# Attention to mixture-of-experts kernel: token rows stored in parts, routing parts moved behind a copy, fills and splits issued later, decay rows on two queues

## The chip, the core and the metric

The kernel runs on one core of one Trainium2 chip. The core has a matrix engine (TensorE, PE in the profile; its weight loads are PEld), a vector engine (VectorE, DVE), an activation engine (ScalarE, ACT), GpSimd (POOL) and a sync engine (SyncE, SP) that mostly issues DMA transfers. Each engine works off its own instructions in order and waits on semaphores for the others. Sixteen DMA engines move data between HBM, SBUF (on-chip memory of 128 partitions) and, for copies between partitions, from SBUF to SBUF. TensorE writes to PSUM. The metric is the device time of one execution in microseconds; less is better.

## What is computed

Attention with a decay, over 4 batches of 8 heads, 576 tokens, head dimension 64; then a mixture of 8 experts in which each token takes the one expert of its largest logit; then a dense feed-forward pair with a leaky ReLU.

```python
scores = scale * np.matmul(q, k.transpose(0, 1, 3, 2))
cum = np.cumsum(np.log(np.clip(f, 0.0001, 1.0)), axis=-1)
decay = cum[:, :, :, None] - cum[:, :, None, :]
scores = np.where(causal, -1000000000.0, scores + decay)
attn = np.exp(scores - np.max(scores, axis=-1, keepdims=True))
attn = attn / (np.sum(attn, axis=-1, keepdims=True) + 1e-09)
x = np.matmul(attn, v)                       # to (2304, 512): tokens x (heads, dim)
logits = x @ w_gate + modality_bias[modality_id]
e_idx = np.argmax(logits, axis=1)            # gate_w: softmax weight of that expert
out[mask] = gate_w[mask, None] * (np.maximum(x[mask] @ w1[e], 0.0) @ w2[e])
h = out @ w_in                               # 512 x 2048
return np.maximum(0.01 * h, h) @ w_out       # 2048 x 512
```

## The kernel before

Everything is float32 in and out. TensorE works on a rounded form (fp32r); where precision is needed a tile is split into a high part, which ScalarE casts, and a low part, which VectorE subtracts, and a product is three products.

**Attention** works on 16 pairs of heads (g = 0 to 15), four pairs to a batch. The queries are cut into five chunks c of up to 128 rows. A loop over the pairs writes the instructions of TensorE, ScalarE, VectorE and SP in a fixed order (`ordered(tc, MS)`), in four steps per pair: `first` (scores of chunks 0 and 1 of pair g, transposes of chunk 3 of pair g-1, and the lower half of the operands of pair g+1, `prep_lo`), `last` (scores of chunk 4; transposes of chunk 4 and the first value product `pv` of pair g-1), `third` (scores of chunk 2, the second value product of pair g-1, transposes of chunks 0 and 1) and `fourth` (scores of chunk 3, loads for later pairs, the upper half of the operands of pair g+2, `prep_hi`, transposes of chunk 2, and `xout`, which brings the result of pair g-1 to token rows). What is moved by DMA per pair, all issued by SP and in this order: the raw q and k (`raw`, L197), v (`vt`, L188), decay rows (L295, L296), `bk<-aq` (L297), `bq<-raw` (L308), `ak<-raw` (L309) and `aq<-aq` (L310). The last four shift halves between partitions; `aq<-aq` overwrites the half that `bk<-aq` of the same pair reads.

A value product writes the one PSUM tile of the pool `psv` (L420); VectorE copies it out (`xu`, L431) before the next value product may write it. The transposed probabilities go through the pool `pst`, three PSUM tiles in turn, which ScalarE empties into `tt` (L405, L415).

**Routing** of a batch starts when its fourth pair is through `xout`. `route` (L462) is a generator: each `next` writes a few small VectorE instructions (largest logit, one-hot `oall`, ranks, gate weight), and `routed(n)` takes n such pieces at fixed places in the steps: three in `last` ahead of the value product, three in `third`, one behind `fourth`, and one more in each of the two steps for g > 12. The last piece stores the batch's token rows (512 values and the reciprocal of the gate sum) to `xs` in HBM, in two DMAs of 1026 and 128 KB (L531, L532).

**The start** (`start`, L219) makes the cumulated decay `agt` on VectorE (L255, L256, L259), copies its rows into the operands of pair 0 by four small DMAs of SP (L263) and stores it for the other pairs (`agd`, L264). GpSimd meanwhile fills buffers of later pairs with constants (L272 to L284).

**Experts.** 25 slots of 128 tokens are gathered from `xs` by expert; `split` (L832) makes high and low parts of the weights of a slot and issues the load of the next slot's. The splits of the first slot (`split(0, 0, k)`, L1042) and the first transposes of tokens (`trx(0)`, L1043) are written ahead of the expert loop, and a scheduler places them among the last attention instructions; `issue_after(lasts[-1].ins)` lets it place the splits behind the last copy of transposes of chunks 0 and 1. **The dense pair** follows (`g1`, `g2`).

Of the kernel before, what the change touches and what calls it, by code (L numbers as in the profile page):

```python
# [73 lines left out]
def fused(ctx: ExitStack, tc, qk0, qk2, vp, f, mid, wg, mb, w1, w2, w_in, w_out, out):  # L74
# [66 lines left out]
    with tc.tile_pool(name="pst", bufs=PST, space=PSUM) as pst:  # L141
# [77 lines left out]
        def start():  # L219
# [40 lines left out]
            for t, r0, c0 in ((bq, 64, 0), (bk, 66, 2)):  # L260
                for i in range(2):
                    o = t[r0 + i:r0 + i + 1].rearrange("r h s -> r (h s)").rearrange("r (p j) -> r p j", p=8)
                    nc.sync.dma_start(o.bitcast(F32), agt[0:8, c0 + i, :].bitcast(F32))  # L263
            nc.sync.dma_start(agd.rearrange("c h (s j) -> (h s) c j", s=4), agt.bitcast(F32))  # L264
            nc.vector.tensor_sub(ak[64:128, 0], kr[64:128, 0], ak[64:128, 0].bitcast(F32))
            nc.vector.scalar_tensor_tensor(bq[0:64, 0], qr[0:64, 0], 0.125, aq[0:64, 0].bitcast(F32), ALU.mult, ALU.subtract)
# [5 lines left out]
            for t in aq4[1:] + bq4[1:]:  # L272
                nc.gpsimd.memset(t.bitcast(F32), 0.0)
            for t in bq4[1:]:
                nc.gpsimd.memset(t[64:68, :, :64].bitcast(F32), 1.0)
            for t in bqs[1:] + bks[1:]:
                nc.gpsimd.memset(t[64:68].bitcast(F32), 1.0)
            nc.gpsimd.memset(idw, 0.0)
            nc.gpsimd.memset(midi, 0)
            nc.gpsimd.tensor_copy(idw[:, :, 0:P], ident.unsqueeze(1).to_broadcast([P, H // 2, P]))  # L280
            nc.gpsimd.tensor_copy(aq4[0][:, :, :64], aq[:, :, 4 * P:].bitcast(F32))
            nc.gpsimd.tensor_copy(bq4[0][:, :, :64], bq[:, :, 4 * P:].bitcast(F32))
            for t in p4s:
                nc.gpsimd.memset(t[:, S:], 0.0)  # L284
# [52 lines left out]
        def exps(g, c, view, nm, pt):  # L337
            for j in range(2):
                nc.scalar.activation(pt[:, j, :], view[:, j, :], AF.Exp, bias=nm[:, j:j + 1], scale=1.0, accum_out=sms[g % 3][:, c, j:j + 1])  # L339
            st[g, c, "p"] = pt  # L340
# [121 lines left out]
        def route(b):  # L462
# [67 lines left out]
            t0 = b * S  # L530
            nc.sync.dma_start(xs[t0:t0 + 4 * P, :].rearrange("(c p) d -> p c d", p=P), x[:, 0:4, :])  # L531
            nc.sync.dma_start(xs[t0 + 4 * P:t0 + S, :], x[:64, 4, :])  # L532
# [91 lines left out]
        lasts = []  # L624
# [7 lines left out]
        def first(g):  # L632
            then = qk01(g) if g < NG else None
            cs = [tr(g - 1, 3, (j, )) for j in range(2)] if g else ()
            if g + 1 < NG:
                prep_lo(g + 1)
            for c in cs:
                c()
# [3 lines left out]
        def last(g):  # L642
            then = qk4(g) if g < NG else None
            if g:
                tr(g - 1, 4, (0, 1))
                routed(3 + (g > 12))
                pv(g - 1, 0)
            if then:
                then()

        def third(g):
# [4 lines left out]
            if then:  # L656
                cs = [tr(g, c, (0, 1)) for c in range(2)]
                then()
                for c in cs:
                    lasts.append(c())  # L660
# [128 lines left out]
    with tc.tile_pool(name="rt2", reuse_waits="tile", bufs=1) as rt2, \  # L789
# [250 lines left out]
        with tc.issue_after(lasts[-1].ins):  # L1040
# [138 lines left out]
```

## Time and profile before

| what | value |
| --- | --- |
| median of 3 runs | 914.2 us (913.07 to 915.13) |
| profiled execution | 911.09 us |
| its span | 909.4 us |
| TensorE busy | 863.0 us (95%) |
| VectorE busy | 629.2 us (69%) |
| ScalarE busy | 526.4 us (58%) |
| GpSimd busy | 141.9 us (16%) |
| mean granted TensorE clock | 0.987 |

All durations below are of the profiled execution, in microseconds from the start of its span. Attention fills roughly the first 230 us, the experts the time up to about 500 us, the dense pair the rest. A line of a timeline names the start, the length, the engine (SPq is SP's DMA queue, the length there is that of the issue), the line of the program, the operation, and the tiles, output first. In brackets stands how long the engine was idle before and what released it. PEclk is the granted clock of TensorE as a share of full speed.

### The profile page before, as it was taken

How to read it: one execution, taken by the hardware profiler on the slowest of the kernel's cores; microseconds unless marked ns; L12 is line 12 of the kernel's file. 1: busy time of each engine (PE TensorE's matmuls, PEld its weight loads, DVE VectorE, ACT ScalarE, POOL GpSimd, SP SyncE). 2: the span in 40 equal slices, each digit the busy share in tenths (PEclk: the TensorE clock that was granted, in tenths of full speed). 3: DMA queues.
4: the chain of work that ended last, by engine and by line, in shares of the span. 5: the costliest groups of instructions: out<-in, count | busy, mean ns of one | idle time of the engine just before them, and what ended most of it. 6: DMA issues, size and time to landing. Idle time of an engine off the chain costs nothing. (4 is left out here: it accounts for less than half of the span.)

```text
span 909.4 us, 14373 instructions
## 1 busy us (share of the span) xinstructions
PE 863.0 (95%) x4733; PEld 710.0 (78%) x4733; DVE 629.2 (69%) x1091; ACT 526.4 (58%) x993; POOL 141.9 (16%) x181
## 2 busy tenths in 40 slices
PE   5999899898979999999999999999999999999995
PEld 3877777776758788888877888888888888888885
DVE  6677768588899999999987364368336943473333
ACT  5877767577768899999986353354223422232221
POOL 5000000000112324454532100000000000001112
PEclk9999999999999999999999999999999999999998
DMA  5776867758338516422231232024000400011111
GB/s 154 221 175 166 210 162 176 200 120 276 74 98 281 155 42 188 132 70 70 84 103 38 83 94 81 1 70 114 2 1 25 136 27 0 1 47 47 47 47 69
DMA packets 32962, 92.91 MB, mean 102 GB/s; under 512 B 7317, under 2 KB 7989, under 8 KB 32882
## 3 DMA queue, kind: packets, MB, share of 16 engines
q1 hardware_dynamic: 28082, 76.71, 29.6%
q0 software_dynamic: 4800, 15.23, 5.3%
q8 instruction: 39, 0.64, 0.3%
q14 instruction: 41, 0.34, 0.1%
HBM read 132.09 MB, written 14.99 MB: 162 GB/s over the span
## 5 line engine op out<-in xcount | busy, mean ns | idle before, releaser
L1085 DVE SCALAR_TENSOR_TENSOR us<-u,us 128x512 f32<-128x512 f32 (+1 forms) x80 | 51.0, 637 | 126.2 <-ACT us L1084 125.6
L1084 ACT COPY us<-u 128x512 f32<-128x512 f32 (+1 forms) x80 | 43.5, 544 | 162.8 <-PE u L1082 162.7
L1082 PE MATMUL u<-fxl,whii 128*128 128x512 f32 (+1 forms) x320 | 118.1, 369 | 0.0
L1082 PE MATMUL u<-fxh,wloi 128*128 128x512 f32 (+1 forms) x320 | 117.9, 368 | 0.0
L1082 PE MATMUL u<-fxh,whii 128*128 128x512 f32 (+1 forms) x320 | 116.8, 369 | 0.7 <-ACT fxh L740 0.7
L1102 PE MATMUL a<-whio,gh 128*128 128x512 f32 x288 | 112.8, 392 | 0.0
L1102 PE MATMUL a<-wloo,gh 128*128 128x512 f32 x288 | 112.3, 390 | 0.0
L1102 PE MATMUL a<-whio,gl 128*128 128x512 f32 x288 | 106.0, 390 | 0.0
L835 DVE TENSOR_TENSOR w1l<-w1r,w1h 128x1024 fp32r<-128x1024 f32 x84 | 100.8, 1221 | 4.6 <-ACT w1h L834 4.1
L835 DVE TENSOR_TENSOR w2l<-w2r,w2h 128x1024 fp32r<-128x1024 f32 x80 | 94.4, 1217 | 0.9 <-ACT w2h L834 0.7
L834 ACT CAST w1h<-w1r 128x1024 fp32r<-128x1024 f32 x84 | 85.8, 1054 | 2.3 <-PE h L854 2.2
L339 ACT ACTIVATE p<-sc,nm 128x128 f32<-128x128 f32 (+3 forms) x128 | 66.1, 526 | 31.3 <-DVE nm L334 28.4
L834 ACT CAST w2h<-w2r 128x1024 fp32r<-128x1024 f32 x80 | 81.4, 1051 | 2.8 <-PE y L882 2.2
L1088 ACT CAST gh<-us 128x512 fp32r<-128x512 f32 (+1 forms) x80 | 46.2, 578 | 58.7 <-DVE us L1085 39.4
L1089 DVE TENSOR_TENSOR gl<-us,gh 128x512 fp32r<-128x512 f32 (+1 forms) x80 | 50.9, 636 | 39.8 <-ACT gh L1088 39.0
L334 DVE TENSOR_REDUCE nm<-sc 128x2 f32<-128x256 f32 (+1 forms) x64 | 51.1, 819 | 30.0 <-PE sc L328 22.5
L882 PE MATMUL y<-w2h,hl 128*128 128x512 f32 x160 | 64.0, 400 | 5.5 <-DVE hl L875 5.4
L1112 POOL DMA_INDIRECT out<-acc,tid x18 | 17.9, 995 | 327.2 <-DVE acc L1109 290.1
L1082 PEld LDWEIGHTS u<-fxh,whii 128*128 128x128 f32 x320 | 60.2, 188 | 11.1 <-ACT fxh L740 0.9
L1082 PEld LDWEIGHTS u<-fxh,wloi 128*128 128x128 f32 x320 | 60.3, 188 | 10.4
L1082 PEld LDWEIGHTS u<-fxl,whii 128*128 128x128 f32 x320 | 60.3, 188 | 10.2
L882 PE MATMUL y<-w2h,hh 128*128 128x512 f32 x160 | 65.3, 408 | 0.0
(263 smaller groups left out, 1839.4 us busy)
## 6 DMA issues: line engine op xcount, KB each, us to landing
w1r<-w SPq DMA_DIRECT2D x88, 512.0 KB
w2r<-w SPq DMA_DIRECT2D x82, 512.0 KB
rwi<-w_in SPq DMA_DIRECT2D x16, 512.0 KB
rwo<-w_out SPq DMA_DIRECT2D x16, 512.0 KB
raw<-qk SPq DMA_DIRECT2D x14, 576.0 KB
vt<-vp SPq DMA_DIRECT2D x16, 320.0 KB
xr<-yd SPq DMA_DIRECT2D x18, 256.5 KB
bk<-aq SPq DMA_DIRECT2D x15, 288.0 KB
```

What stands on the lines that cost most here:

```text
L334: nc.vector.tensor_reduce(nm, view, axis=AX.X, op=ALU.max, negate=True)
L339: nc.scalar.activation(pt[:, j, :], view[:, j, :], AF.Exp, bias=nm[:, j:j + 1], scale=1.0, accum_out=sms[g % 3][:, c, j:j + 1])
L834: nc.scalar.copy(hi[k], raw[k])
L835: nc.vector.tensor_tensor(lo[k], raw[k], hi[k].bitcast(F32), ALU.subtract)
L882: nc.tensor.matmul(Yp[t], lhsT=ap[:, k * P:(k + 1) * P], rhs=wp[k // 2][:, k % 2, :], start=(k == 0 and i == 0), stop=(k == NFB - 1 and i ...
L1082: nc.tensor.matmul(ps, lhsT=w[:, c], rhs=x[:, k, :], start=(k == 0 and i == 0), stop=(k == NKB - 1 and i == 2))
L1084: nc.scalar.copy(us, ps)
L1085: nc.vector.scalar_tensor_tensor(us, ps, 0.01, us, ALU.mult, ALU.max)
L1088: nc.scalar.copy(gh, us)
L1089: nc.vector.tensor_sub(gl, us, gh.bitcast(F32))
L1102: nc.tensor.matmul(A[b][i], lhsT=x[:, c], rhs=w, start=(first and m == 0), stop=(last and m == 2))
L1112: d = nc.gpsimd.indirect_dma_start(out=out[:, :], out_offset=bass.IndirectOffsetOnAxis(ap=tid[:, c:c + 1], axis=0), in_=Y[b, i], in_offset ...
```

## The change

- **Stores.** The last routing piece no longer stores. It puts the parts of the batch on a list: chunks 0 and 1, 2 and 3, and 4 for the batches 0 and 1; chunks 0 to 3, and 4 for the others. `store(1)`, or `store(2)` for g > 12, issues from the list in `first`, behind `prep_lo` of the next pair. The last batch is stored at once.
- **Routing pieces.** In `last` one piece stays ahead of the value product and the others go behind it.
- **Fills.** GpSimd's two copies into the operands of pair 0 come ahead of the fills for later pairs, and the fills may be placed only behind VectorE's L266 (`d`).
- **Decay rows.** The two small DMAs into `bk` are issued by ScalarE, the two into `bq` still by SP.
- **Splits.** Those of the first slot may be placed only behind the last exponentials.

```diff
-                    nc.sync.dma_start(o.bitcast(F32), agt[0:8, c0 + i, :].bitcast(F32))
+                    (nc.sync if t is bq else nc.scalar).dma_start(o.bitcast(F32), agt[0:8, c0 + i, :].bitcast(F32))
...
-            nc.vector.scalar_tensor_tensor(bq[0:64, 0], qr[0:64, 0], 0.125, aq[0:64, 0].bitcast(F32), ALU.mult, ALU.subtract)
+            d = nc.vector.scalar_tensor_tensor(bq[0:64, 0], qr[0:64, 0], 0.125, aq[0:64, 0].bitcast(F32), ALU.mult, ALU.subtract)
...
-            for t in aq4[1:] + bq4[1:]:
-                nc.gpsimd.memset(t.bitcast(F32), 0.0)
...
             nc.gpsimd.tensor_copy(aq4[0][:, :, :64], aq[:, :, 4 * P:].bitcast(F32))
             nc.gpsimd.tensor_copy(bq4[0][:, :, :64], bq[:, :, 4 * P:].bitcast(F32))
-            for t in p4s:
-                nc.gpsimd.memset(t[:, S:], 0.0)
+            with tc.issue_after(d.ins):
+                for t in aq4[1:] + bq4[1:]:
+                    nc.gpsimd.memset(t.bitcast(F32), 0.0)
...
+                for t in p4s:
+                    nc.gpsimd.memset(t[:, S:], 0.0)
...
-            t0 = b * S
-            nc.sync.dma_start(xs[t0:t0 + 4 * P, :].rearrange("(c p) d -> p c d", p=P), x[:, 0:4, :])
-            nc.sync.dma_start(xs[t0 + 4 * P:t0 + S, :], x[:64, 4, :])
+            for c in ((0, 2), (2, 4), (4, 5)) if b < B - 2 else ((0, 4), (4, 5)):
+                stores.append((b, x, *c))
+            if b == B - 1:
+                store(2)
+
+        stores = []
+
+        def store(n):
+            for _ in range(min(n, len(stores))):
+                b, x, c0, c1 = stores.pop(0)
+                t0 = b * S + c0 * P
+                if c0 == 4:
+                    nc.sync.dma_start(xs[t0:(b + 1) * S, :], x[:64, 4, :])
+                else:
+                    nc.sync.dma_start(xs[t0:t0 + (c1 - c0) * P, :].rearrange("(c p) d -> p c d", p=P), x[:, c0:c1, :])
...
                 prep_lo(g + 1)
+            store(1 + (g > 12))
...
                 tr(g - 1, 4, (0, 1))
-                routed(3 + (g > 12))
+                routed()
                 pv(g - 1, 0)
+                routed(2 + (g > 12))
...
-        with tc.issue_after(lasts[-1].ins):
+        with tc.issue_after(st["exp"].ins):
```

**Order on SP, batch 0.** `xs<-x` is a store of token rows, `aq<-aq` the last transfer of a pair, `raw` and `vt` the loads of a later one. Before, in the steps of pair 6:

```order
L310 DMA aq_1151<-aq_1151 64x1152
L531 DMA xs<-x_203 128x4x513
L532 DMA xs<-x_203 64x513
L197 DMA raw_1324<-qk 128x1152
L188 DMA vt_1326<-vp 128x640
L295 DMA bq_167<-agd 2x1152
L295 DMA bk_169<-agd 2x1152
L296 DMA bq_175<-agd 2x2x64
L297 DMA bk_169<-aq_1328 64x1152
```

In the changed kernel, in the steps of pair 7 (the next part stands at the same place of pair 8, the rest at that of pair 9):

```order
L309 DMA bq_167<-raw_1147 64x1152
L310 DMA ak_1327<-raw_1147 64x1152
L311 DMA aq_1326<-aq_1326 64x1152
L545 DMA xs<-x_203 128x2x513
L197 DMA raw_1478<-qk 128x1152
L188 DMA vt_1480<-vp 128x640
L296 DMA bq_168<-agd 2x1152
L296 DMA bk_170<-agd 2x1152
L297 DMA bq_176<-agd 2x2x64
L298 DMA bk_170<-aq_1482 64x1152
```

The store of 1026 KB that stood in one piece ahead of a pair's loads is now a store of 513 KB ahead of the loads of each of two pairs, and each stands one place behind `aq<-aq`.

**Order on VectorE, a pair with routing** (batch 0; `eq`, `m` and `oall` are routing, `xu` the copy of the value product). Before:

```order
L475 TENSOR_REDUCE mx_1069<-lgs 128x5
L478 TENSOR_TENSOR eq_1071<-lgs,mx_1069 128x40
L479 TENSOR_TENSOR eq_1071<-eq_1071,rev 128x40
L482 TENSOR_REDUCE m_1074<-eq_1071 128x5
L484 TENSOR_TENSOR oall<-eq_1071,m_1074 128x40
L431 COPY xu_1084<-pv_0_1077 128x384
L334 TENSOR_REDUCE nm_2_1094<-sc_2_1087 128x2
```

In the changed kernel:

```order
L476 TENSOR_REDUCE mx_1069<-lgs 128x5
L432 COPY xu_1079<-pv_0_1072 128x384
L479 TENSOR_TENSOR eq_1071<-lgs,mx_1069 128x40
L480 TENSOR_TENSOR eq_1071<-eq_1071,rev 128x40
L483 TENSOR_REDUCE m_1083<-eq_1071 128x5
L485 TENSOR_TENSOR oall<-eq_1071,m_1083 128x40
L335 TENSOR_REDUCE nm_2_1094<-sc_2_1087 128x2
```

The copy moved ahead of four instructions; the reduction behind it keeps its place.

**Order on ScalarE, end of the attention stage** (`w1h<-w1r` are the splits' casts, `p_3` the last exponentials, `tt` the copies of transposes, `xh` the cast of the first slot's tokens). Before:

```order
L834 CAST w1h_129<-w1r_119 128x1024
L834 CAST w1h_130<-w1r_120 128x1024
L834 CAST w1h_131<-w1r_121 128x1024
L834 CAST w1h_132<-w1r_122 128x1024
L415 COPY tt_0_2846<-pt_2_0_2869 128x3x128
L415 COPY tt_0_2846<-pt_2_1_2873 128x3x128
L339 ACTIVATE p_3_2894,sm_178<-sc_3_2860,nm_3_2867 128x512 x2
L415 COPY tt_1_2897<-pt_3_0_2898 128x4x128
L843 CAST xh_133<-tx_3173 128x512
L415 COPY tt_1_2897<-pt_3_1_2903 128x4x128
L405 COPY tt_1_2897<-pt_4_0_2910 128x2x3x64
L405 COPY tt_1_2897<-pt_4_3_2915 128x2x2x64
```

In the changed kernel:

```order
L416 COPY tt_0_2848<-pt_2_0_2871 128x3x128
L416 COPY tt_0_2848<-pt_2_1_2875 128x3x128
L340 ACTIVATE p_3_2896,sm_178<-sc_3_2862,nm_3_2869 128x512 x2
L848 CAST w1h_129<-w1r_119 128x1024
L848 CAST w1h_130<-w1r_120 128x1024
L848 CAST w1h_131<-w1r_121 128x1024
L848 CAST w1h_132<-w1r_122 128x1024
L416 COPY tt_1_2899<-pt_3_0_2900 128x4x128
L416 COPY tt_1_2899<-pt_3_1_2905 128x4x128
L406 COPY tt_1_2899<-pt_4_0_2912 128x2x3x64
L857 CAST xh_133<-tx_3175 128x512
L406 COPY tt_1_2899<-pt_4_3_2917 128x2x2x64
```

The four casts moved behind two copies and the exponentials, and the token cast behind two more copies. On TensorE the token transposes (`tx`) moved from behind the first half of the transposes of chunk 3 to between the two groups of chunk 4 (three transposes and two); on VectorE the four subtractions of the splits moved behind the scaling of pair 14's rows (`xout`).

## Rows read from the trace of the kernel before

**Rows 1.** TensorE waits, 20 to 240 us; who waited for whom: us in total, times, longest

```profile
PE sc L325 <- DMA aq<-aq: 5.5, 2, 3.6
PE pv L425 <- DVE xu L431: 4.1, 8, 0.8
```

**Rows 2.** Stretches, pair by pair: length, busy us (instructions) per engine, PEclk, DMA share, GB/s

```profile
60.22:72.28 12.06, 11.83 (x102) 9.51 (x100) 8.47 (x17) 9.52 (x28) 0.86 (x3) 1.00 0.71 195
98.77:112.63 13.86, 11.88 (x102) 9.60 (x100) 9.82 (x22) 11.39 (x32) 1.25 (x5) 1.00 0.94 209
112.63:125.95 13.32, 13.32 (x98) 11.10 (x99) 6.60 (x10) 7.56 (x24) 0.29 (x1) 0.87 0.75 218
152.43:167.87 15.44, 11.89 (x101) 9.60 (x100) 9.88 (x22) 11.49 (x32) 1.24 (x5) 1.00 0.90 185
167.87:181.20 13.33, 13.33 (x98) 11.13 (x99) 6.52 (x9) 7.38 (x23) 0.29 (x1) 0.87 0.75 221
220.00:232.00 12.00, 8.93 (x66) 7.35 (x65) 8.54 (x16) 9.29 (x17) 1.99 (x2) 0.86 0.41 163
```

**Rows 3.** Timeline, pairs 6 to 8: start, length, what, [idle before it and its releaser]

```profile
96.30 0.39 SPq L531 DMA_DIRECT2D xs<-x  x1
100.96 0.47 SPq L297 DMA_DIRECT2D bk<-aq  x1
109.35 0.46 SPq L310 DMA_DIRECT2D aq<-aq  x1
112.63 0.30 PE L325 MATMUL sc<-ak,aq 128*128 128x128 f32 x1 [1.98 <-DMA aq<-aq]
```

**Rows 4.** Timeline, queue of SP, a pair without stores

```profile
86.22 0.47 SPq L297 DMA_DIRECT2D bk<-aq  x1
92.08 0.74 SPq L310 DMA_DIRECT2D aq<-aq  x1
```

**Rows 5.** Stretches of one microsecond in that pair, columns as in rows 2

```profile
86.00:87.00 1.00, 1.00 (x12) 0.95 (x11) 0.80 (x5) 0.98 (x5) 0.58 (x2) 1.00 0.04 15
89.00:90.00 1.00, 1.00 (x10) 0.83 (x9) 1.00 (x2) 0.53 (x4) 0.00 (x0) 1.00 0.07 16
```

**Rows 6.** Timeline, pair 13: VectorE routing piece and the second value product

```profile
187.60 0.20 DVE L478 TENSOR_TENSOR eq<-lgs,mx 128x40 f32<-128x40 f32 x1
189.12 1.64 PE L425 MATMUL pv<-tt,vt 128*64 128x192 f32 x20 [0.68 <-DVE xu L431]
```

**Rows 7.** Timeline, the start, in order of time

```profile
5.56 0.36 DVE L254 TENSOR_SCALAR p<-p,off 128x144 f32<-128x144 f32 x1
5.95 0.92 DVE L255 CAST agt<-p 128x144 fp32r<-128x144 f32 x1
7.25 0.96 DVE L259 TENSOR_SCALAR agt<-agt 128x288 fp32r<-128x288 f32 x1
7.99 1.21 POOL L277 MEMSET bk<- 4x1152 f32 x1
8.60 1.31 SPq L263 DMA_DIRECT2D bk<-agt  x2
12.57 0.47 PE L325 MATMUL sc<-ak,aq 128*128 128x128 f32 x1 [0.73 <-DVE ak L271]
13.30 0.29 POOL L281 CAST aq<-aq 128x128 fp32r<-128x128 f32 x1
17.14 0.49 SPq L308 DMA_DIRECT2D bq<-x  x1
```

**Rows 8.** Timeline, end of the attention stage

```profile
218.91 3.88 ACT L834 CAST w1h<-w1r 128x1024 fp32r<-128x1024 f32 x4
222.70 0.86 ACT L415 COPY tt<-pt 128x384 f32<-128x384 f32 x2
223.23 1.32 PE L448 MATMUL xo<-idw,xub 128*128 128x144 f32 x4 [2.31 <-ACT tt L415]
229.78 1.64 PE L425 MATMUL pv<-tt,vt 128*64 128x192 f32 x20 [0.75 <-DVE xu L431]
```

More of the change, by code (lines that the diff above doesn't have):

```diff
@@ L271, in start @@
             nc.vector.tensor_sub(ak[64:128, 1], kr[64:128, 1], ak[64:128, 1].bitcast(F32))
-            for t in aq4[1:] + bq4[1:]:
-                nc.gpsimd.memset(t.bitcast(F32), 0.0)
[L274 to L280, printed above, removed]
             nc.gpsimd.tensor_copy(aq4[0][:, :, :64], aq[:, :, 4 * P:].bitcast(F32))
             nc.gpsimd.tensor_copy(bq4[0][:, :, :64], bq[:, :, 4 * P:].bitcast(F32))
-            for t in p4s:
-                nc.gpsimd.memset(t[:, S:], 0.0)
+            with tc.issue_after(d.ins):
+                for t in aq4[1:] + bq4[1:]:
+                    nc.gpsimd.memset(t.bitcast(F32), 0.0)
+                for t in bq4[1:]:
+                    nc.gpsimd.memset(t[64:68, :, :64].bitcast(F32), 1.0)
+                for t in bqs[1:] + bks[1:]:
+                    nc.gpsimd.memset(t[64:68].bitcast(F32), 1.0)
+                nc.gpsimd.memset(idw, 0.0)
+                nc.gpsimd.memset(midi, 0)
+                nc.gpsimd.tensor_copy(idw[:, :, 0:P], ident.unsqueeze(1).to_broadcast([P, H // 2, P]))
+                for t in p4s:
+                    nc.gpsimd.memset(t[:, S:], 0.0)
             ops[0] = (aq, bq, ak, bk)
@@ L338, in exps @@
             for j in range(2):
-                nc.scalar.activation(pt[:, j, :], view[:, j, :], AF.Exp, bias=nm[:, j:j + 1], scale=1.0, accum_out=sms[g % 3][:, c, j:j + 1])
+                st["exp"] = nc.scalar.activation(pt[:, j, :], view[:, j, :], AF.Exp, bias=nm[:, j:j + 1], scale=1.0, accum_out=sms[g % 3][:, c, j:j + 1])
             st[g, c, "p"] = pt
@@ L623, in fused @@
         routing = []
-        lasts = []
         def routed(n=1):
@@ L659, in third @@
                 for c in cs:
-                    lasts.append(c())
+                    c()
         def fourth(g):
```

## Prediction

> **What bounds the kernel now.** I first read the list of TensorE's waits, cut to the attention stage [rows 1]. TensorE is the busy engine there, and the list says what stops it: 5.5 us in two waits for the transfer `aq<-aq`, the longer 3.6, and 4.1 us in eight waits for the copy `xu` on VectorE. Next I read busy time by stretch, one stretch per pair of heads, from the first score matmul of a pair to that of the next [rows 2]. An undisturbed pair takes 12.06 us with TensorE busy for 11.83, so a microsecond that TensorE waits is a microsecond of the stage. Four pairs are longer: 13.86 and 15.44 us, each holding one of the two long waits, and behind each a pair of 13.32 or 13.33 us with TensorE busy throughout, in which the granted clock is 0.87: a part of the pair ran at the lower of the two levels (1.2 instead of 2.4 GHz) after TensorE had stood still. Last I read the queue of SP in order of time [rows 3]. The token rows of a batch go out at 96.30; the copy `bk<-aq` of the next pair is issued at 100.96, behind these rows and two loads; `aq<-aq` overwrites what that copy reads, so SP issues it only at 109.35, and the matmul at 112.63 waited 1.98 us for it. The second batch repeats this with the longer wait. In a pair without stores `bk<-aq` goes out at 86.22 and `aq<-aq` at 92.08 [rows 4].
>
> **Stores in parts.** The same bytes are moved, with one DMA more for each of the batches 0 and 1. What moves is their place: a store of two chunks (513 KB) now stands behind `aq<-aq` of a pair, two pairs in a row, and the small rest behind the third. Three things follow. SP no longer stands at the store until the routing has finished, since the store comes a pair later. `aq<-aq` and its neighbours are ahead of the store. And the next `bk<-aq` has half as many bytes ahead of it. Does that do? The DMA engines were busy for 0.71 x 12.06 = 8.6 us of the undisturbed pair and for 0.94 x 13.86 + 0.75 x 13.32 = 23.0 us of the two pairs with a store [rows 2], so the whole store cost about 23.0 - 17.1 = 5.9 us of them and a part of 513 KB costs about 2.6 (an estimate from these rows). In the pair without stores the engines were nearly idle from 86 to 87 us (0.04), then carried `bk<-aq`, issued at 86.22, and were idle again from 89 (0.07) [rows 4, 5]; the next `aq<-aq` goes out at 92.08. Put 2.6 us of store ahead: the engines are free by about 88.5 instead of 86, `bk<-aq` takes 2 us and lands by about 90.5, ahead of 92.08 by 1.6 us. So both waits should go, and with them the slow clock behind them. Worth: the four long pairs less four undisturbed ones, 13.86 + 13.32 + 15.44 + 13.33 - 4 x 12.06 = **7.7 us**. Other engines don't eat it: VectorE and ScalarE are busy for under 10 of the 12.06 us. If half of the waiting remains, 3.9 are left.
>
> **Routing parts behind the copy.** In a pair with routing VectorE worked off three pieces before it copied `xu`, and the second value product, which needs that PSUM tile, waited: 0.68 us at 189.12 [rows 6], the longest within the three batches. Of the eight waits in [rows 1] one, 0.75 us at 229.78, has no routing ahead of it and stays [rows 8]; the other seven are 4.1 - 0.75 = **3.3 us**. At 189.12 four instructions like that of 187.60, 0.20 us each, move behind the copy, more than the 0.68 us to be had. What they delay is not late: VectorE's next reduction needs scores that end after them either way. TensorE reaches the transposes behind it 0.7 us sooner, and it had no wait listed there, so I take the whole 3.3, and keep 2.0 as the low end (the three longest waits alone).
>
> **Start: fills held back, two queues.** VectorE's `agt` cast of 144 columns took 0.92 us and the negation of 288 took 0.96, with GpSimd fills beside them; the operation of 144 columns just ahead took 0.36 [rows 7]. By that row the two should take about 0.4 and 0.45, so 1.05 us. What VectorE gains reaches TensorE at its third score matmul, 12.57, which waited for VectorE. The Trainium skill, SBUF — State Buffer, "Who interferes with whom", says that GpSimd and a two-port VectorE operation hold a shared port pair in turn, each for a whole instruction; these rows agree. By the same rule the two GpSimd casts now put ahead of the fills may block VectorE in their turn; with 0.29 us for each [rows 7] the gain would be 0.5 and the whole sum 0.5 us smaller. The second queue takes two issues (1.31 us for such a pair on SP) off SP, so the store of decay rows goes out that much sooner; ScalarE now stands until the negation is done and then issues, and its two casts for the second head come later by about a microsecond. Their reader on VectorE comes after four other operations, so I cost that at nothing; if an issue on ScalarE takes twice SP's 0.65 us, about 1 us of the gain goes. The fills end later: from about 11 us on, against SP's loads of decay rows for the next pair, which now wait for two fills, the longer 1.21 us, until about 15. What follows them on SP, 17.14, waits for VectorE anyway (16.1 with the gain), so about a microsecond of cover is left. I take **1.0 us**, with 0 to 1.3 as bounds.
>
> **Splits behind the last exponentials.** Before, four casts of expert weights (3.88 us) ran on ScalarE ahead of two copies (0.86 us), and TensorE waited 2.31 us for these [rows 8]. Now they run behind the copies and the exponentials, from about 222.3 to 226.1, and ahead of the copies of the last transposes. The wait moves: the projection at 223.23 goes at about 221; but the last two of the five transposes of chunk 4 need a PSUM buffer that is freed by a copy behind the casts, at about 226.6, so TensorE stands from about 224.1. ScalarE's work to that point is the same, and the second value product, 229.78, comes at about 229.4 by its chain (ScalarE's cast `xh`, VectorE's `xl`, then `xu`). Against these 0.4 us stands the clock: after each of the stops of 2.0, 3.6 and 2.3 us the granted clock was lower [rows 2], and after a stop of 2.5 I expect it again, now under the value products that everything waits for. It cost 13.3 - 12.06 = 1.3 us a time in rows 2. I take a **loss of 0.6 us**, bounds a gain of 0.4 and a loss of 2.
>
> **Sum.** -7.7 - 3.3 - 1.0 + 0.6 = -11.4 us. Behind the attention stage the order of the engines is unchanged and no load there starts at a fixed time, so the gain is carried through. The profiled execution took 911.1 us (span 909.4), the median of the runs is 914.2. 911.1 becomes 899.7; taken off the median it is **902.8 us**. Its own range: a gain of 9 to 13.5, 900.7 to 905.2.
>
> **Rivals.** (1) *The queue stays too long.* The parts fill four pairs instead of two; if `bk<-aq` still lands late in some of them, half of the 7.7 us stays: 906.7. For it: with a part the engines are busy for 8.6 + 2.6 of 12.06 us, a share of 0.93. Against: the slack of 1.6 us worked out above. (2) *The gain is given back at the end of attention.* Should the value products stand for the whole of the casts, 3.9 us less 0.4 instead of 0.6, the sum is -8.5: 905.7. Against: ScalarE did the same casts ahead of the same products before. (3) *The small edits do nothing*, since another wait is just behind each: without 3.3 and 1.0 the sum is -7.1, 907.1. (4) *Slower: each of the four big parts stalls as the whole store did.* Place: `aq<-aq` of the pair behind each part, waiting for `bk<-aq`. Price: 7.7 / 2 = 3.9 us for each of four, 15.4 instead of 7.7, so +7.7 - 3.3 - 1.0 + 0.6 = +4.0: 918.2. It decides when a part takes 1.6 us more of the queue than I estimate, 4.2 instead of 2.6; the whole store took 5.9. (5) *The row tile.* A batch is written into the tile of the batch two before, whose last part now goes out behind `aq<-aq`, only about half a pair ahead of that write; should it land late, VectorE and then TensorE stand twice, 1 to 2 us each: about 905.8.
>
> **How the numbers follow.** Main line 902.8 with 0.68; rival 1 0.12, rival 2 0.07, rival 3 0.05, rival 4 0.04, rival 5 0.04. The range reaches from 899.5 (the full 1.3 at the start, a gain of 0.4 at the end, and 2 us for slow stretches of the clock that the runs around the median may hold beyond the profiled one) to 907.2, which takes in rivals 1, 2, 3 and 5 at their central times and leaves out rival 4 and the tails of the others. A measurement of this kernel can tell about 0.2% (1.8 us) from no change; all but rival 4 lie beyond that on the fast side, and I leave 0.02 for the middle: faster 0.94, same 0.02, slower 0.04.
>
> **What would show it.** Right: no wait of TensorE for `aq<-aq`; the four long pairs at 12 to 12.4 us with a granted clock of 1.00; the waits for `xu` down to one; the third score matmul near 11.5 us; TensorE's stop at the end of attention behind the casts, at the last transposes of chunk 4, followed by a lower clock; all stages behind it as long as before. Wrong: SP waiting at `aq<-aq` for `bk<-aq` in the pairs with a part; SP waiting for the fills beyond the time when VectorE's `raw` is ready; ScalarE's casts of the second head later than VectorE's use; a stage behind attention that grows.

## The result, and the profile after

The changed kernel takes 900.4 us (median of 6 runs, 899.3 to 905.1); the kernel before took 913.6 (911.3 to 915.1) on the same chip. The ratio is 0.9863, 95% interval 0.9841 to 0.9886, so the gain is 12.5 us with bounds of 10.4 and 14.5. The forecast was a gain of 11.4 and 902.8 us, with a range of 899.5 to 907.2.

The profiled execution of the changed kernel is the longest of its six: 905.05 us, span 903.3, mean granted clock 0.981. The same program, run once more in a later experiment (`again`), left a profile of 900.62 us, span 898.9, clock 0.992. Both are used below, since where they differ no step of the program does. The spans of the two profiles are 6.1 and 10.5 us shorter than the span before, and neither shows the whole of the 12.5: the profile before is of a run of 911.09 us, 2.5 below the median of its kernel. What the slower runs of the kernel before lose beyond that profile stands in no trace.

The spans, cut at the first score matmul of a pair as in [rows 2], and at the first expert product (`h`, L854 before, L868 after):

| stretch | before | after | `again` | forecast of the change |
| --- | --- | --- | --- | --- |
| start to pair 1 | 23.41 | 23.31 | 23.10 | -1.0 |
| pairs 1 to 4 | 48.87 | 51.13 | 50.00 | 0 |
| pairs 5, 6, 9, 10 (routing) | 52.97 | 50.98 | 51.00 | part of -3.3 |
| pairs 7, 8, 11, 12 (the four long ones) | 55.95 | 48.30 | 47.33 | -7.7 |
| pairs 13, 14 (routing of the third batch) | 25.73 | 24.12 | 24.97 | part of -3.3 |
| pair 15 to the first `h` | 25.65 | 27.52 | 25.48 | +0.6 |
| behind it | 676.82 | 677.94 | 677.02 | 0 |
| span | 909.40 | 903.30 | 898.90 | -11.4 |

The gain stands where the forecast put it, in the four long pairs and the pairs with routing. Pairs 1 to 4 and the end of attention differ between the two profiles of one program by 1.1 and 2.0 us.

TensorE's waits of the changed kernel, 20 to 240 us (columns as in [rows 1], which these lines answer):

```profile
PE sc L326 <- DMA aq<-aq: 2.5, 2, 1.8
...
PE pv L426 <- DVE xu L432: 0.8, 1, 0.8
```

The eight waits for `xu` are down to one. The wait for `aq<-aq` is not gone, but the longer of the two that remain stands at pair 1, where the profile before has none. Its length depends on the execution: in `again` it is 0.48 us, because TensorE came to that point 1.1 us later. One more wait is new, for the gather of the first slot's tokens (`xg`, 1.9 us, shown below).

Stretches of the changed kernel, columns as in [rows 2]: pair 1, the four pairs that were long (7, 8, 11, 12), and a piece of the end of attention.

```profile
23.31:38.11 14.80, 14.80 (x99) 12.57 (x99) 7.57 (x12) 8.87 (x26) 0.86 (x3) 0.77 0.82 247
...
99.95:111.58 11.63, 11.63 (x102) 9.53 (x100) 7.76 (x15) 9.19 (x28) 0.65 (x3) 1.00 0.73 175
111.58:123.62 12.04, 11.82 (x102) 9.52 (x100) 8.45 (x17) 9.49 (x28) 0.86 (x3) 1.00 0.83 212
149.09:160.72 11.63, 11.63 (x102) 9.53 (x100) 7.76 (x15) 9.19 (x28) 0.65 (x3) 1.00 0.76 177
160.72:173.72 13.00, 12.07 (x101) 9.58 (x100) 9.32 (x20) 10.46 (x31) 1.23 (x5) 1.00 0.83 213
...
218.00:224.00 6.00, 5.25 (x31) 3.53 (x28) 1.30 (x3) 2.09 (x4) 0.99 (x1) 0.50 0.14 35
```

Three of the four long pairs are now undisturbed ones, all at a granted clock of 1.00; the fourth ends with a short wait. The DMA share of a pair with a part is 0.73 to 0.83, not 0.94 and 0.90. Elsewhere this execution has slow stretches: pair 1 has a clock of 0.77, and at the end of attention the clock is 0.50, which is the lower level, for six microseconds of value products.

SP's queue in pairs 7 and 12, and the matmul that starts pair 13 (start, length, what; it answers [rows 3]):

```profile
99.64 0.47 SPq L298 DMA_DIRECT2D bk<-aq  x1
...
105.01 0.78 SPq L311 DMA_DIRECT2D aq<-aq  x1
105.83 1.16 SPq L545 DMA_DIRECT2D xs<-x  x1
...
166.53 0.78 SPq L311 DMA_DIRECT2D aq<-aq  x1
...
173.72 0.30 PE L326 MATMUL sc<-ak,aq 128*128 128x128 f32 x1 [0.71 <-DMA aq<-aq]
```

SP's wait at `aq<-aq` for `bk<-aq` to land, 20 to 210 us (who waited for whom: us in total, times, longest), before and after:

```profile
SPq L310 <- DMA bk<-aq: 9.9, 4, 3.5
```

```profile
SPq L311 <- DMA bk<-aq: 2.5, 3, 1.6
```

`aq<-aq` is issued 5.4 us behind `bk<-aq` (99.64 to 105.01); in the long pair before it was 8.4 (100.96 to 109.35). In pair 12 it went out 5.4 us behind `bk<-aq` too (161.16 to 166.53), and the matmul that needs it started 7.2 us later.

The start of the changed kernel, in order of time (it answers [rows 7]):

```profile
5.95 0.23 DVE L255 CAST agt<-p 128x144 fp32r<-128x144 f32 x1
...
6.56 0.31 DVE L259 TENSOR_SCALAR agt<-agt 128x288 fp32r<-128x288 f32 x1
...
6.95 1.89 ACTq L263 DMA_DIRECT2D bk<-agt  x2
...
7.71 0.47 PE L326 MATMUL sc<-ak,aq 128*128 128x128 f32 x1 [2.70 <-DVE ak L265]
...
11.64 0.48 PE L326 MATMUL sc<-ak,aq 128*128 128x128 f32 x1 [0.22 <-DVE ak L271]
...
13.11 1.05 POOL L280 MEMSET bq<- 4x1152 f32 x1
...
14.18 0.28 SPq L296 DMA_DIRECT2D bq<-agd  x1
...
15.80 0.55 SPq L298 DMA_DIRECT2D bk<-aq  x1
...
16.45 0.54 SPq L309 DMA_DIRECT2D bq<-x  x1
...
19.17 0.46 SPq L311 DMA_DIRECT2D aq<-aq  x1
...
23.31 0.44 PE L326 MATMUL sc<-ak,aq 128*128 128x128 f32 x1 [1.81 <-DMA aq<-aq]
```

Pair 0 starts at 7.71 instead of 9.05 and its third score matmul at 11.64 instead of 12.57, as forecast. Pair 1 starts at 23.31 instead of 23.41: almost nothing of it is left. SP's decay rows for pair 1 stood behind the fill of 13.11 and the one after it, `bk<-aq` went out at 15.80 instead of 13.50, and `aq<-aq`, which overwrites what it reads, at 19.17 instead of 18.38. The lines of the kernel before:

```profile
13.50 0.55 SPq L297 DMA_DIRECT2D bk<-aq  x1
...
18.38 0.76 SPq L310 DMA_DIRECT2D aq<-aq  x1
```

One profile would not carry this, but the same start was profiled six times (`after`, `again`, `a_start`, `whole`, `late`, `no_splits`): pair 1 starts at 23.02 to 23.89 there, and at 23.41 to 23.46 in the four profiles with the start of before. In all six it starts 4.1 us behind the issue of `aq<-aq`.

The end of attention, in the changed kernel (it answers [rows 8]):

```profile
212.02 3.88 ACT L848 CAST w1h<-w1r 128x1024 fp32r<-128x1024 f32 x4
...
215.02 1.11 PE L856 MATMUL tx<-ident,xg 128*128 128x128 f32 x4 [1.86 <-DMA xg<-xs,gidx]
216.44 0.69 PE L404 MATMUL pt<-ident,p 128*128 128x128 f32 x2 [0.30 <-ACT tt L416]
217.05 2.83 PE L426 MATMUL pv<-tt,vt 128*64 128x384 f32 x12
220.64 3.04 PE L426 MATMUL pv<-tt,vt 128*64 128x192 f32 x20 [0.75 <-DVE xu L432]
```

and in `again`:

```profile
213.88 0.65 PE L856 MATMUL tx<-ident,xg 128*128 128x128 f32 x4 [2.15 <-DMA xg<-xs,gidx]
...
215.50 2.83 PE L426 MATMUL pv<-tt,vt 128*64 128x384 f32 x12
219.08 1.64 PE L426 MATMUL pv<-tt,vt 128*64 128x192 f32 x20 [0.75 <-DVE xu L432]
```

and in `no_queue`, a kernel of a later experiment whose program is the same at this place:

```profile
215.56 0.66 PE L857 MATMUL tx<-ident,xg 128*128 128x128 f32 x4 [2.08 <-DMA xg<-xs,gidx]
216.75 0.44 PE L404 MATMUL pt<-ident,p 128*128 128x128 f32 x2 [0.53 <-ACT tt L416]
217.11 1.52 PE L426 MATMUL pv<-tt,vt 128*64 128x384 f32 x12
219.38 1.64 PE L426 MATMUL pv<-tt,vt 128*64 128x192 f32 x20 [0.75 <-ACT w2h L849]
```

The stop is the same in all three, 2.2 to 2.6 us in two pieces: the casts on ScalarE with the gather inside their time. Behind it the two value products take 2.83 and 3.04 us, 2.83 and 1.64, or 1.52 and 1.64, which is the full clock. Whether the lower clock follows, and for how long, differs between executions.

### The profile page after: what moved, and what is told of

It reads as the page before. It is cut to its first block, busy times and chain, and to the rows that moved or that the text cites. A ratio compares the mean times of both kernels' runs of the same rounds, so it can differ in the third digit from the quotient of the medians.

```text
span 903.3 us, 14379 instructions
## 1 busy us (share of the span) xinstructions
PE 863.2 (96%) x4733; PEld 707.9 (78%) x4733; DVE 627.2 (69%) x1091; ACT 525.2 (58%) x993; POOL 139.2 (15%) x181
## 5 line engine op out<-in xcount | busy, mean ns | idle before, releaser
L1096 PEld LDWEIGHTS u<-fxh,wloi 128*128 128x128 f32 x320 | 60.3, 188 | 10.4
```

The lines of the kernel that those rows point to most:

```text
L1096: nc.tensor.matmul(ps, lhsT=w[:, c], rhs=x[:, k, :], start=(k == 0 and i == 0), stop=(k == NKB - 1 and i == 2))
```

## The experiments

### Each part alone

Four kernels with one part of the change each on the kernel before, compared with it on one chip (914.6 us). The theory is the forecast's sum, term by term; its rivals are that the small edits do nothing (rival 3) and that half of the queue's waiting stays (rival 1).

`a_stores`: the token rows in parts behind `aq<-aq`.

```diff
-            nc.sync.dma_start(xs[t0:t0 + 4 * P, :].rearrange("(c p) d -> p c d", p=P), x[:, 0:4, :])
...
+            for c in ((0, 2), (2, 4), (4, 5)) if b < B - 2 else ((0, 4), (4, 5)):
+                stores.append((b, x, *c))
...
+            store(1 + (g > 12))
```

> The kernel before with the stores in parts alone. Theory (my first term): both long waits of TensorE for aq<-aq and the slow clock behind them go, -7.7 us, about 906 us against 913.6. Rival (the queue stays too long): SP still waits at aq<-aq for bk<-aq in the pairs with a part, -3.9 us or less, 909.7 or more. The trace of the whole change shows one such wait of 0.7 us, so I expect at least -6.5.

Measured: 905.1 us, ratio 0.9894 (0.9863 to 0.9925), a gain of 9.7 us (6.9 to 12.5). The four long pairs take 11.63, 12.04, 11.62 and 12.74: 48.03 instead of 55.95. TensorE's wait for `aq<-aq` is down to one:

```profile
174.67 0.30 PE L325 MATMUL sc<-ak,aq 128*128 128x128 f32 x1 [0.44 <-DMA aq<-aq]
```

This part alone is most of the change, by the mechanism forecast. The traces differ by less than the times: the span is 6.6 us shorter than the one before, and the profile before is, as said, of a run below the median.

`a_copy`: one routing piece ahead of the value product, the others behind its copy.

```diff
-                routed(3 + (g > 12))
+                routed()
                 pv(g - 1, 0)
+                routed(2 + (g > 12))
```

> The kernel before with the routing pieces behind the copy alone. Theory: seven waits of TensorE for xu go, -3.3 us, about 910.3. Rival: the waits are taken up by something just behind, or the long waits for aq<-aq grow by what TensorE gains (the transfer's time is set by SP and the DMA queue, not by TensorE): then only the waits in pairs without a long wait behind them count, -1 to -2 us, 912.

Measured: 910.5 us, ratio 0.9961 (0.9941 to 0.9982), a gain of 3.6 us (1.6 to 5.4). TensorE's waits in it (20 to 240 us) show the copy's wait at its one unrelated place, and the queue's wait, which this edit does not touch, still there and now three times:

```profile
PE sc L325 <- DMA aq<-aq: 6.8, 3, 3.5
PE xo L448 <- DVE lp L452: 3.6, 1, 3.6
...
PE pv L425 <- DVE xu L431: 0.8, 1, 0.8
```

The third wait for `aq<-aq` is at pair 1:

```profile
23.42 0.30 PE L325 MATMUL sc<-ak,aq 128*128 128x128 f32 x1 [0.89 <-DMA aq<-aq]
```

This kernel has the start of the kernel before, and pair 1 starts where it did there (23.41). So with the old start too `aq<-aq` holds pair 1 until then, if TensorE is early enough to wait. The second line shows what the edit costs at the end of attention: the stop at the projection is 3.6 us there, for VectorE, where it was 2.31, for ScalarE [rows 8]. The stretch from pair 15 to the first `h` is 25.96 us, before 25.65.

`a_start`: the fills held back and the decay rows issued from two queues.

```diff
-                    nc.sync.dma_start(o.bitcast(F32), agt[0:8, c0 + i, :].bitcast(F32))
+                    (nc.sync if t is bq else nc.scalar).dma_start(o.bitcast(F32), agt[0:8, c0 + i, :].bitcast(F32))
...
+            with tc.issue_after(d.ins):
+                for t in aq4[1:] + bq4[1:]:
...
```

> The kernel before with the held-back fills and the decay rows on two queues. My prediction: -1.0 us. What the trace of the whole change says instead: the third score matmul comes 0.9 us sooner, but SP waits 3.7 us for the fills of pair 1's rows, bk<-aq goes out 2.3 us later and aq<-aq of pair 1 with it, so pair 1 starts where it started before, and a slow clock can follow the new stop of 1.8 us. By that: 0 to +2 us, 913.6 to 915.6. The two expectations differ by 1 to 3 us.

Measured: 913.1 us, ratio 0.9992 (0.9971 to 1.0012): no difference that can be told, though the interval takes in a gain of 1.0 as well. Pair 0 starts at 7.71 and takes 15.63 us instead of 14.36; pair 1 starts at 23.34. SP's waits in its first 10 to 24 us (who waited for whom: us in total, times, longest) name the places:

```profile
SPq L296 <- POOL bq L280: 3.7, 1, 3.7
...
SPq L311 <- DMA bk<-aq: 1.3, 1, 1.3
```

Before, SP waited there 0.2 us for GpSimd and not at all for `bk<-aq`. TensorE's own wait at pair 1, 2.2 us, is put down to ScalarE's exponentials in this profile. In `again` the same matmul starts at 23.10 while those exponentials run until 24.4, so it does not need them; `aq<-aq` is what is left.

`a_splits`: the splits of the first slot behind the last exponentials.

```diff
...
-        with tc.issue_after(lasts[-1].ins):
+        with tc.issue_after(st["exp"].ins):
```

> The kernel before with the splits of the first slot behind the last exponentials alone. My prediction: +0.6 us (bounds -0.4 to +2). The trace of the whole change shows the stretch from the start of pair 15 to the first expert product at 27.5 us against 25.65 before, with the slow clock under the value products: by that +1.9, 915.5. Rival: the slow clock was a matter of that one execution, and the median shows 0.

Measured: 915.0 us, ratio 1.0007 (0.9986 to 1.0027), a loss of 0.6 that can't be told from nothing. The stretch from pair 15 to the first `h` takes 26.63 us, before 25.65.

The four gains together make 13.4 us, the whole change 12.5: within the intervals the parts add up.

### Place or size of the stores

`whole` is the changed kernel with each batch's four chunks in one store of 1026 KB again, at the new place.

```diff
-            for c in ((0, 2), (2, 4), (4, 5)) if b < B - 2 else ((0, 4), (4, 5)):
+            for c in ((0, 4), (4, 5)):
```

> The changed kernel with the store of batches 0 and 1 at its new place but in one part of 1026 KB (and the rest in the pair behind). Theory of place (what counts is that aq<-aq no longer stands behind the store and the routing): within 1 us of the changed kernel's 900.4. Theory of size, from the prediction's slack of 1.6 us against 5.9 - 2.6 = 3.3 us more in the queue: bk<-aq lands about 1.7 us after the next pair wants it, SP waits for it at aq<-aq in two pairs, and of the 3.9 us that each of the two places gave, up to 2 us go: 901.5 to 904.

Measured: 903.2 us, ratio 0.9867 (0.9847 to 0.9886); the changed kernel had 0.9863 and 0.9847 in its two experiments. By the median that lies in the range of the theory of size; the kernel before beside it was slower too, and the ratio taken off the 913.6 of the first experiment makes 901.5, between the two theories. The queue does show the whole store: SP's waits (20 to 210 us) first, then TensorE's in pairs 2 to 15 (30 to 200 us).

```profile
SPq L311 <- DMA bk<-aq: 11.9, 5, 4.5
```

```profile
PE sc L326 <- DMA aq<-aq: 1.6, 2, 1.2
```

SP stands at `aq<-aq` for `bk<-aq` as it did before, up to 4.5 us. But `bk<-aq` behind the first store goes out 0.44 us into its pair (111.74, pair 7 starting at 111.30 there), where it was 2.19 before (100.96, [rows 3], pair 7 starting at 98.77), since SP no longer stood at the store for the routing. (In the old place SP also stood at `bq<-raw` until the store had landed, 3.2 and 4.8 us, here 0.2; that wait ended before the one for `bk<-aq`.) Only 1.6 us of the waiting reaches TensorE, and the two pairs it falls on, 12.65 and 13.50 us, are followed by pairs of 12.12 and 12.07: no lower clock behind them. So what the change gains here it gains by the place, behind `aq<-aq` and no longer ahead of it; the smaller size takes off what is left, 0.5 to 0.6 us in the traces (pairs 7 to 14 take 98.37 us, in the changed kernel 97.89 and 97.79) and nothing that the times can tell.

### The start

`rowfill` is the changed kernel with only the fills of pair 1's one-rows early again, beside VectorE's L259.

```diff
-            nc.vector.tensor_scalar(agt[:, 2:4, :], agt[:, 0:2, :].bitcast(F32), -1.0, None, ALU.mult)
+            neg = nc.vector.tensor_scalar(agt[:, 2:4, :], agt[:, 0:2, :].bitcast(F32), -1.0, None, ALU.mult)
...
+            with tc.issue_after(neg.ins):
+                for t in bqs[1:] + bks[1:]:
+                    nc.gpsimd.memset(t[64:68].bitcast(F32), 1.0)
             nc.gpsimd.tensor_copy(aq4[0][:, :, :64], aq[:, :, 4 * P:].bitcast(F32))
...
-                for t in bqs[1:] + bks[1:]:
-                    nc.gpsimd.memset(t[64:68].bitcast(F32), 1.0)
```

> The changed kernel with the two fills that SP waits for (the constant rows of pair 1's bq and bk) put ahead of GpSimd's two copies and behind VectorE's negation, the other fills as in the changed kernel. Theory (SP's wait of 3.7 us for a fill delays bk<-aq and so aq<-aq of pair 1): SP's loads go out about 3 us sooner, TensorE's wait of 1.8 us at pair 1 goes, -1.5 us, -3 where a slow clock had followed, 898 to 899. Rival (aq<-aq of pair 1 is late for its place in the DMA queue behind the first loads): the same time, 900.4. The scheduler also moves one product across the rank products in the first expert slot here; I count that as nothing.

Measured: 901.5 us, ratio 0.9860 (0.9841 to 0.9880). Its start:

```profile
6.58 0.79 DVE L259 TENSOR_SCALAR agt<-agt 128x288 fp32r<-128x288 f32 x1
...
10.55 0.28 SPq L297 DMA_DIRECT2D bq<-agd  x1
...
13.77 0.55 SPq L299 DMA_DIRECT2D bk<-aq  x1
...
17.64 0.76 SPq L312 DMA_DIRECT2D aq<-aq  x1
...
22.74 0.45 PE L327 MATMUL sc<-ak,aq 128*128 128x128 f32 x1
```

The fill costs VectorE's L259 0.48 us (0.79 instead of 0.31) and pair 0 half a microsecond, and brings the queue forward by 3.6, 2.0 and 1.5 us; pair 1 starts 0.57 us sooner than in the changed kernel. The two other kernels with these early fills (`best`, `late_rf`) start pair 1 at 22.74 and 22.64, below all six profiles of the changed start. So the fills ahead of SP's decay rows were what took the start's gain back, 0.7 us of it against the kernel before. More was not to be had by this alone: in `late_rf` TensorE is there early and waits 1.39 us for `aq<-aq`. The time of the whole does not show the gain, neither the 898 to 899 of the theory nor a difference from the changed kernel: in this profile the end of attention took 28.05 us.

`no_queue` is the changed kernel with all four small DMAs of decay rows on SP.

```diff
-                    (nc.sync if t is bq else nc.scalar).dma_start(o.bitcast(F32), agt[0:8, c0 + i, :].bitcast(F32))
+                    nc.sync.dma_start(o.bitcast(F32), agt[0:8, c0 + i, :].bitcast(F32))
```

> The changed kernel with all four small DMAs of decay rows issued by SP again, as before the change. If the second queue is what brings the first pair forward, pair 0 starts 0.5 us later or more (8.2 instead of 7.71); if the fills' place alone does it (VectorE's L255 and L259 at 0.23 and 0.31 us instead of 0.92 and 0.96), pair 0 starts within 0.3 us of 7.71. In both cases `bk<-aq` of pair 1 goes out at about 15.8, because the queue stands behind a GpSimd fill, and the total is within 1 us of the changed kernel's: pair 1, not pair 0, is what the rest follows.

Measured: 901.2 us, ratio 0.9854 (0.9831 to 0.9877), beside 0.9847 for the changed kernel in the same comparison.

```profile
7.75 0.47 PE L326 MATMUL sc<-ak,aq 128*128 128x128 f32 x1 [2.72 <-DVE ak L265]
...
11.99 0.48 PE L326 MATMUL sc<-ak,aq 128*128 128x128 f32 x1 [0.80 <-DVE ak L271]
```

Pair 0 starts where it did, so the fills' place alone brings it forward. A gain by the second queue isn't shown. The third score matmul comes 0.35 us later here, but in the six profiles with the second queue it lies between 11.38 and 12.22. VectorE's L294 ahead of it waits for the load of pair 1's q and k, 0.24 to 1.08 us in them and 0.82 here; the matmul starts 2.32 us behind L294 in all of them, so the landing of that load makes the difference. The times show nothing either.

### The end of attention

`no_splits` is the changed kernel with the splits placed as before; `best` is that with the early fills of `rowfill`.

```diff
...
-        with tc.issue_after(st["exp"].ins):
+        with tc.issue_after(lasts[-1].ins):
```

> The changed kernel with the splits of the first slot placed as in the kernel before (behind the last copy of transposes of chunks 0 and 1). Prediction's term: 0.6 us faster than the changed kernel, 899.8. What the traces say: the stretch from pair 15 to the first expert product falls from 27.5 to about 25.7 us, because the slow clock no longer lies under the value products: 898.5. Rival: the splits' place is neutral (the kernel before with the splits alone moved: +0.6 with -1.3 to +2.5), 900.4.

> The changed kernel with both: the two row fills early and the splits placed as before. Sum of the two theories: 1.5 to 3 and 0.6 to 1.9 us, 895.5 to 898.3. Rival (both neutral): 900.4.

Measured: 902.0 us, ratio 0.9860 (0.9840 to 0.9879), and 900.9 us, ratio 0.9846 (0.9831 to 0.9862). Neither kernel shows the gain that its theory names. The stretch from pair 15 to the first `h` is 26.62 and 26.85 us. In the five profiles that have the change's place of the splits and its other parts at this point it is 24.35 (`no_queue`), 25.48 (`again`), 26.88 (`whole`), 27.52 and 28.05 (`rowfill`). Both `no_splits` and `best` have their stop at the projection, 3.6 us behind VectorE, as `a_copy` has. Neither place of the splits is better by what the runs can tell; `best` did not beat the changed kernel by more than its interval.

Both places have the casts ahead of copies that TensorE waits for. So `late` holds the splits until ScalarE's last copy of the transposes of chunk 4, and `late_rf` adds the early fills. In both the scheduler also puts `tx` behind the two value products.

```diff
-                    nc.scalar.copy(sb[:, :, b0:b1, P:], i)
+                    st["t4"] = nc.scalar.copy(sb[:, :, b0:b1, P:], i)
...
-        with tc.issue_after(st["exp"].ins):
+        with tc.issue_after(st["t4"].ins):
```

> The changed kernel itself once more, so that the three others of this call can be set against it on one chip. Median near 901 us, ratio near 0.986; in the profile the stretch from pair 15 to the first expert product near 26.5 to 27.5 us, with TensorE's stop of about 1.9 us for the gather `xg` at `tx` wherever the clock stood.

> The changed kernel with the splits behind the last copy of the transposes of chunk 4, the fills as in the changed kernel. Theory A: 2 to 4 us below the changed kernel run beside it (897 to 899 us); theory B: within 1 us of it. Against the run with the fills moved too it shows what the fills are worth with nothing else different: 0.6 us by the earlier start of pair 1 (22.74 against 23.31), nothing if the end of attention takes it back.

> The changed kernel with two edits: the splits of the first slot may come only behind the last copy of the transposes of chunk 4 (in place of the last exponentials), and the two fills of one-rows of pair 1 come ahead again, beside VectorE's L259. Theory A (the end of attention is long because the casts stand ahead of the copies that TensorE needs, and `tx` stands ahead of the value products and waits for its gather): both stops ahead of the value products go, `pv` 0 starts near 214.5 instead of 217 and runs 1.64 us, not 2.8; the stretch from pair 15 to the first expert product falls from 27.5 to 22 to 24 us, total 896 to 899 us. Theory B (the weights' low parts on VectorE are what the first expert product really stands behind): the subtractions now come among the copies and scalings of the last pair, TensorE waits there instead, the stretch stays at 26 to 28 us, total 900 to 902 us.

Measured, on one chip beside a kernel before of 914.0: `again` 900.1 us, ratio 0.9847 (0.9823 to 0.9871); `late` 900.1, ratio 0.9840 (0.9817 to 0.9863); `late_rf` 897.7, ratio 0.9824 (0.9801 to 0.9848). The end of `late_rf`:

```profile
210.47 1.51 PE L427 MATMUL pv<-tt,vt 128*64 128x384 f32 x12
212.74 1.64 PE L427 MATMUL pv<-tt,vt 128*64 128x192 f32 x20 [0.75 <-DVE xu L433]
...
218.43 0.73 PE L869 MATMUL h<-w1h,xl 128*128 128x512 f32 x2 [0.89 <-DVE xl L859]
```

The value products run at full clock, and the stretch from pair 15 to the first `h` falls to 21.82 us in both kernels, at a granted clock of 1.00 (the row is `late_rf`'s, columns as in [rows 2]):

```profile
194.99:216.81 21.82, 19.99 (x175) 15.73 (x174) 16.36 (x48) 16.66 (x40) 2.24 (x2) 1.00 0.72 255
```

So theory A names the wait: with the casts behind the copies that TensorE needs, both stops ahead of the value products are gone. What the casts cost in the changed kernel is 2.5 us where no lower clock followed (24.35 in `no_queue` less 21.82, and the stop there is 2.6), and up to 6.2 where it did (28.05). The `late` kernels move `tx` as well; it was not the last thing waited for, since in all three profiles above the transposes behind it wait again, for ScalarE's copy.

Theory B has a part too. TensorE waits for `xub` and `xl` behind the subtractions, 0.57 and 0.89 us, and the second of these waits stands behind the first `h`, where the stretch does not count it. From pair 15 to the end of the span `late` takes 700.5 us and `late_rf` 699.3, `no_queue` 702.3, `again` 702.5 and the profile after 705.5: of the 3.7 us by which the stretch is shorter than in `again`, 2.0 and 3.2 are left at the end.

The times follow less clearly. `late_rf` is the fastest kernel of the study by its median, 2.4 us below `again`, with intervals that overlap; `late` has the same median as `again`, where its expectation by theory A was 2 to 4 us lower. Against the profile of `again` that of `late` loses 1.1 us in pair 1 (14.78 instead of 13.67) and 1.7 behind the first `h`; whether all its runs did is not shown by one profile.

## Why the prediction was right, point by point

**Stores, -7.7.** Right in mechanism; the term was right or a little small. The four pairs fell by 7.7 and 8.6 us in the two profiles and by 7.9 in `a_stores`, whose times say 9.7 with an interval that takes in the forecast. The forecast took 12.06 us for a pair without a wait; three of the four are at 11.63 to 12.04. The slack worked out for `bk<-aq` was there (SP's wait for it at `aq<-aq` fell from 9.9 us to 2.5, in `again` 3.1, and none of it is left in the four pairs). That no wait of TensorE for `aq<-aq` would remain was wrong by 0.4 to 0.7 us at pair 13 in these profiles (in `again` by 0.2, at pair 14): there the transfer itself took long, not the one ahead. The forecast's sum counted half of the store's size; `whole` shows that the place would have done nearly all of it. Rival 4 (each part stalls) and rival 1 (half remains) needed `bk<-aq` late in several pairs; even the whole store, behind which SP waited up to 4.5 us for it, cost TensorE only 1.6 us. Rival 5 (the row tile) did not show: in the profile after VectorE waits for no store of token rows between 20 and 240 us.

**Routing behind the copy, -3.3.** Right: 3.6 us in `a_copy`, one wait for `xu` left, of 0.75 us, at the place that was named [rows 8]. "What they delay is not late" missed the end of attention, where the stop at the projection grew by 1.3 us with this edit alone.

**Start, -1.0.** The first step held: the casts took 0.23 and 0.31 us (estimated at 0.4 and 0.45), and the third score matmul came at 11.64. The step that failed is "What follows them on SP, 17.14, waits for VectorE anyway". It is true of `bq<-raw`, which went out at 16.45; but `aq<-aq`, two places behind, waits for `bk<-aq` to land, and `bk<-aq` went out 2.3 us later. The prediction names just this dependence where it speaks of the stores, and did not apply it at the start. Nor was there cover without the fills: `a_copy` waits for `aq<-aq` at pair 1 with the start of before, so what TensorE gains at its third score matmul ends at that transfer unless the transfer comes sooner too. In place of a gain of 1.0 at pair 1 the six profiles show from 0.4 sooner to 0.5 later, and `a_start` made no difference that can be told. The start's half of rival 3 came true. What the prediction feared of GpSimd's two casts did not: from L265 on, none of VectorE's operations on the way to the third score matmul is longer than before by more than 0.02 us. Of the 1.3 us by which VectorE was ahead, 0.24 to 1.08 went into its wait for the load of pair 1.

**Splits, +0.6.** The place of the stop and its length (2.2 to 2.6 us in two pieces, forecast 2.5) came as forecast; the lower clock under the value products came in four of the five profiles named above and not in `no_queue`. The size depends on the execution: against the 25.65 of before, from -1.3 to +2.4 in these five and +1.0 in `a_splits`, whose times say 0.6 (-1.3 to 2.5). Two of the five lie outside the bounds given, and no run shows the 0.6 itself. That `tx` would wait there for its gather was not foreseen; it costs little, since the transposes behind it wait for the copies behind the casts until 216.4 either way.

**The sum.** -11.4 forecast, -12.5 measured. The start was over-sized by about 0.9 us; against it stand up to 0.9 us more from the stores in the traces and 2.0 by the times of `a_stores`. That the sum came out within 1.1 us owes something to errors of opposite sign, and 2 us of the 12.5 stand in no trace. The stages behind the first `h` took 677.9 and 677.0 us, before 676.8: the gain was carried through, as the prediction said.

**What stays open.** Pairs 1 to 4 were 1 to 2 us longer in the changed kernel's profiles, but pair 1 took 13.93, 14.12 and 14.00 us in `a_stores`, `a_copy` and `a_splits` too, whose start is that of the kernel before, and 12.80, 12.60 and 12.77 in the kernel before, in `a_start` and in `late_rf`. It is not one cause: in the changed kernel's two profiles TensorE is busy throughout pair 1 (14.80 and 13.67 us) and its matmuls are slow, while in `a_copy` it is busy for 12.04 of the 14.12 and waits for ScalarE's copies. What decides between these is not settled.

## What to carry to other kernels

A large store belongs behind the queue's last transfer that someone waits for; put there, its size mattered little here. When work is moved past a queue, follow every wait of that queue to the next matmul, the landing of an earlier transfer among them, and not only the instruction next in line. Where an engine works for two stages at a change of stage, look for the place behind the last thing the old stage needs of it (`late`, 21.82 us), and not only for another place in between (24.35 to 28.05), and measure to a point behind the moved work, since a part of the gain is paid back there.

## What was unexpected

- `aq<-aq` of 288 KB landed 3.3 us after its issue in the long pair before [rows 3], and 7.2 us after it at pair 13 of the changed kernel, with two transfers of 288 KB issued within 1.2 us ahead of it and the part of the store and two loads right behind it. The same neighbours cost no wait at pairs 8, 9 and 12. At the start the matmul that needs it comes 5.05 us behind its issue where `ak<-x` went out 0.7 us ahead (`a_copy`), and 4.1 where SP's wait put 2.1 us between them. Which of the neighbours makes it slow at pair 13 was not tried.
- Stops of one length were followed by different stretches at the lower clock in executions of one program: at the end of attention 2.83 and 3.04 us for the two value products in one profile, 2.83 and 1.64 in the other, and no such stretch in `no_queue`. A difference of 2 us between two single profiles of this kernel says nothing of an edit.
- VectorE's L259 took 0.96 us beside GpSimd fills, 0.79 beside one fill (`rowfill`), 0.31 alone. The Trainium skill, SBUF — State Buffer, "Who interferes with whom", says that a two-port VectorE operation and GpSimd block each other for a whole instruction; these three values agree.
- The two small DMAs into `bk` took 1.89 us to issue on ScalarE, against 1.31 for the same pair on SP in `no_queue` and before [rows 7]; no gain of the second queue can be told.
